# Another order of the steps in a linear-attention and feed-forward kernel

## The chip, the cores and the metric

One core of a Trainium2 chip runs the whole program. The metric is the device time of that core in microseconds (us). Five engines work side by side, each through its own list of instructions in a fixed order: PE (TensorE: matrix products; its weight loads are shown as PEld), DVE (VectorE), ACT (ScalarE), POOL (GpSimd) and SP (SyncE, which issues nearly all DMAs here). An instruction that waits holds up everything behind it on its engine.

## The reference

```python
# attention: q, k, v, alpha of shape (4, 8, 768, 48)
for t in range(S):
    state = alpha[:, :, t, :, None] * state + einsum('bhd,bhe->bhde', k[:, :, t], v[:, :, t])
    y[:, :, t] = einsum('bhd,bhde->bhe', q[:, :, t], state)
# feed-forward: x = y as (3072 tokens, 384); w_in (384, 2048), w_out (2048, 384)
h = x @ w_in
sp = maximum(h, 0.0) + log1p(exp(-abs(h)))
out = (h * erf(sp)) @ w_out
```

The inputs are float64; the result is float32.

## The kernel before, in words

The 768 positions are cut into 12 chunks of 64. A chunk holds 64 positions of all four batches, 256 tokens, and after the attention of a chunk a feed-forward block of the same number works on its 256 tokens. The work is written as named steps; a step is a generator, and each time that its name comes in the table `SCHED` it issues one piece. Names end in numbers: `y_1` is step `y` of chunk 1; `H_7_2_0` is step `H` of block 7, group 2, half 0; `wi_5` and `wo_5` are tile 5 of `w_in` and of `w_out` (16 tiles each).

Attention steps of chunk n:
- `la`, `lk`, `lq`, `lv` load alpha, keys, queries and values (SP). `kx`, `qx` copy rows of K and Q to a fourth block (SP, line 236).
- `a1` is the running product of alpha (DVE, L353); `ln`, `ex`, `gd` take its logarithm, its inverse and a range check (ACT); `w1`, `w2`, `w3`, `a3` scale K and Q (DVE).
- `s` multiplies queries with keys (PE, L414) and masks the result into `sT` (DVE). `t` turns the keys (PE, L434) and copies them into `kn` (line 211 on ACT or 213 on DVE); `u` adds keys times values to the state `T` (PE L462, DVE L470).
- `lv`/`tx` and `qc`/`sx` gather values with state into W and queries with `sT` into X by DMA (L301, L334, L314, L324). `y` multiplies X with W (PE, L504) and writes the block's input: `x_hi` by a copy, `x_lo` as the rest.

Feed-forward steps of block n, for four groups of four tiles each:
- `H` is `x @ w_in` in three products of high and low halves, 12 and then 6 matmuls (L590), and a copy of the PSUM bank into `hs`. Block 0 instead takes `w_in` whole in fp32 (L579).
- `U`, `L1` (three), `G` are five ACT instructions on 128x1024 values; `U` and `G` need another table of functions than `L1`, `ln` and `ex`, and each change costs an ACT_TABLE_LOAD (L204). `L2` and `Z` are two DVE instructions each.
- `O` copies the result to `gh` (ACT or DVE), makes `gl` (DVE), and then issues 12, 12, 6 and 6 matmuls with `w_out` (L660) that add to two PSUM banks `acc`. `out` copies these and sends them off.

A weight tile arrives as float64 in a buffer `wst`, and steps `wi`, `wo` of seven pieces each turn it into a high and a low float32 half: one DMA, a copy and a shift (mostly ACT, L211 and L710), two DVE instructions (L714, L718), the copy to `wi_hi` or `wo_hi`, and the DVE subtraction to `wi_lo` or `wo_lo` (L726).

What sets the order: `steps()` walks through `SCHED` and issues piece by piece, and PE, ACT, DVE and SP keep exactly that order. A prefix `v:` puts a copy of that piece on DVE instead of ACT (for a third piece of `wi` or `wo` it is the other way: the shift goes to ACT). Big tiles share 24 buffers of 4 KB per partition, PSUM is eight banks; a piece waits until its buffer is free.

Of the kernel before, what the change touches and what calls it, by code (L numbers as in the profile page):

```python
# [44 lines left out]
a3_1 wi_6 qx_1 H_0_0_1 wi_13 wi_14 v:wi_14 w3_2 wi_15 wi_9 wi_6 wi_2 wi_1 wi_7 wi_14 wi_6 H_0_1_0 H_0_0_0 wi_0 t_2
U_0_0 u_0 v:wi_9 wi_14 wi_14 kx_2 a3_2 wi_7 wi_12 wi_12 wi_6 wi_8 wi_13 v:wi_13 u_0 wi_2 s_1 wi_8 s_1 H_0_1_1 wi_10
qx_2 H_0_3_1 s_1 wi_9 wi_13 v:wi_12 wi_12 wi_13 v:wi_8 wi_8 wi_5 s_2 lv_1 wi_10 H_0_1_0 v:wi_10 wi_7 H_0_1_1 v:wi_13
wi_7 wi_12 t_2 v:t_2 wi_11 tx_1 wi_8 wi_10 sx_1 qc_1 wi_14 U_0_1 wi_12 wi_12 v:wi_8 wi_9 wi_8 wo_9 la_3 wi_11 v:wi_11
u_1 L1_0_1 s_2 wi_11 wi_10 wi_13 L1_0_0 wi_11 L1_0_0 H_0_3_0 wo_4 v:H_0_3_0 wi_10 s_2 wo_5 u_1 L1_0_0 L1_0_1 H_0_2_0
L2_0_0 a1_3 wi_11 y_1 wi_10 y_1 y_1 y_1 wi_9 H_0_2_1 wi_9 wo_3 wo_0 L1_0_1 H_0_2_0 wo_9 v:wo_9 H_1_0_0 ln_3 H_1_3_0  # L50
sx_2 wi_11 wo_9 H_0_2_1 y_1 wo_5 qc_2 wo_9 wo_3 H_1_1_0 H_1_1_1 L2_0_1 ex_3 y_1 H_1_0_0 L2_0_0 H_0_3_1 lv_2 wo_4
L2_0_1 tx_2 v:wo_5 wo_5 G_0_0 H_1_1_0 H_1_1_0 G_0_1 H_1_1_1 wo_0 H_1_2_1 v:wo_4 w1_3 H_1_1_1 H_1_3_0 y_2 wo_5 wo_5
w2_3 v:wo_3 v:wo_0 lk_3 Z_0_1 wo_2 u_2 w3_3 Z_0_0 lq_3 wo_3 wo_15 wo_4 y_2 a3_3 H_1_3_0 H_1_0_0 U_0_3 wo_4 wo_3 Z_0_1
wo_15 wo_0 t_3 t_3 t_3 H_1_0_1 y_2 y_2 v:wo_15 wo_4 wo_3 u_2 kx_3 wo_2 wo_1 wo_4 wo_1 y_2 y_2 wo_6 qx_3 wo_3 wo_15
v:wo_1 L1_0_3 H_1_2_1 H_1_0_1 H_1_2_0 H_1_3_1 wo_9 wo_5 H_1_2_0 s_3 lv_3 u_3 la_4 tx_3 wo_14 wo_1 v:wo_2 v:H_1_0_1
wo_6 wo_1 H_1_2_0 H_2_2_0 s_3 wo_6 s_3 wo_0 wo_9 wo_1 wo_1 qc_3 H_1_3_1 L1_0_3 wo_6 wo_15 H_1_2_1 Z_0_0 H_2_0_0
H_1_3_1 L1_0_3 H_2_2_1 H_2_1_1 O_0_1 u_3 sx_3 H_2_2_0 wo_0 wo_14 v:wo_14 wo_0 U_1_0 wo_8 L2_0_3 G_0_3 wo_10 wo_15
H_2_0_0 y_3 H_2_2_0 y_3 wo_6 O_0_0 L2_0_3 a1_4 wo_10 v:wo_10 wo_15 H_2_3_1 wo_2 H_2_1_1 H_2_0_0 y_3 O_0_0 Z_0_3 U_0_2
wo_7 wo_2 wo_14 wo_7 v:wo_7 wo_7 wo_13 O_0_0 wo_10 H_2_2_1 H_2_2_1 y_3 H_2_0_1 H_2_3_1 wo_2 H_3_2_1 y_3 wo_2 wo_8 gd_3
wo_14 y_3 wo_6 wo_13 O_0_0 wo_11 v:wo_8 la_5 wo_10 lk_4 Z_0_3 v:wo_10 v:wo_11 v:wo_11 H_3_2_1 wo_7 O_0_1 wo_10 H_2_0_1  # L60
ln_4 wo_8 wo_6 O_0_0 H_2_1_0 L1_0_2 H_3_2_1 wo_7 ex_4 wo_7 ends_3 wo_11 wo_14 H_2_3_1 w1_4 v:wo_13 wo_13 wo_8 H_2_3_0
w2_4 lq_4 H_3_3_1 wo_13 L1_0_2 O_0_0 H_3_2_0 L1_1_0 a3_4 O_0_1 ends_3 w3_4 L1_0_2 H_3_2_0 wo_13 wo_14 L1_1_0 wo_13
O_0_1 L2_0_2 H_3_2_0 qx_4 wo_12 H_2_3_0 L1_1_0 H_3_3_0 H_2_1_0 O_0_1 wo_11 wo_8 wo_8 L2_0_2 u_3 H_3_3_0 kx_4 H_2_0_1
H_2_3_0 v:wo_12 G_0_2 Z_0_2 O_0_1 H_3_3_1 H_2_1_0 wo_11 wo_11 qc_4 v:wo_12 t_4 lv_4 H_2_1_1 H_3_3_1 Z_0_2 L2_1_0 U_1_1
tx_4 s_4 s_4 s_4 O_0_2 H_3_0_1 O_0_2 O_0_2 H_3_0_0 L2_1_0 H_3_3_0 wo_12 G_1_0 L1_1_1 t_4 Z_1_0 L1_1_1 t_4 O_0_2 wo_12
H_3_0_1 O_0_3 O_0_2 Z_1_0 u_4 L1_1_1 U_2_0 sx_4 y_4 v:wo_12 O_0_3 U_1_3 H_3_0_0 O_0_2 y_4 wo_12 L2_1_1 u_4 O_0_3 O_1_0
L2_1_1 lk_5 a1_5 G_1_1 O_1_0 y_4 O_1_0 O_0_3 v:y_4 Z_1_1 U_1_2 O_1_0 la_6 O_0_3 lq_5 O_1_0 ln_5 tx_5 v:H_3_0_1 O_0_3
L1_1_3 ex_5 L1_1_2 O_1_0 Z_1_1 O_1_1 w1_5 L1_2_0 out_0_1 H_4_0_0 y_4 y_4 w2_5 O_1_1 w3_5 O_1_1 L1_2_0 H_4_2_1 out_0_1
O_1_1 H_4_2_1 v:out_0_0 out_0_0 L1_1_2 H_4_2_0 L1_2_0 L1_1_2 a3_5 qx_5 L2_2_0 L2_1_2 L2_2_0 L1_1_3 L1_1_3 L2_1_2
H_4_0_0 G_1_2 U_2_2 lv_5 L2_1_3 H_3_0_0 kx_5 O_1_1 H_4_2_0 H_4_2_0 G_1_3 H_4_0_1 O_1_1 t_5 v:H_4_2_1 s_5 Z_1_2 v:t_5  # L70
t_5 Z_1_2 u_5 U_2_1 s_5 G_2_0 s_5 Z_2_0 H_4_0_1 O_1_2 L2_1_3 H_3_1_0 H_3_1_1 u_5 qc_5 Z_1_3 L1_2_2 L1_2_1 O_1_2 O_1_2
H_4_3_0 H_3_1_1 H_4_3_0 sx_5 H_3_1_0 Z_1_3 L1_2_2 O_1_2 L1_2_2 H_4_0_0 L1_2_1 L1_2_1 H_4_0_1 Z_2_0 y_5 v:H_3_1_0
L2_2_2 H_3_1_1 O_2_0 U_3_1 y_5 L2_2_2 v:H_4_3_0 v:O_1_3 L2_2_1 G_2_2 H_4_1_1 U_3_0 lq_6 O_1_2 G_2_1 H_4_1_1 O_2_0
O_2_0 O_1_2 U_2_3 L1_2_3 y_5 L1_2_3 L2_2_1 O_2_0 Z_2_1 Z_2_1 O_1_3 O_1_3 L1_3_0 y_5 O_2_0 O_1_3 v:O_2_1 O_2_1 y_5
L1_3_0 L1_3_0 H_4_3_1 O_1_3 Z_2_2 v:H_4_1_1 O_2_0 L1_2_3 Z_2_2 H_4_3_1 a1_6 O_2_1 L1_3_1 L1_3_1 O_1_3 H_5_2_0 O_2_1
out_1_0 L1_3_1 y_5 L2_2_3 U_3_3 H_4_3_1 H_5_2_0 L2_3_0 H_5_2_1 O_2_2 H_4_1_0 L2_3_1 G_3_0 O_2_1 out_1_0 H_5_3_0 G_3_1
G_2_3 L2_3_0 v:out_1_1 Z_3_0 L2_2_3 O_2_1 O_2_2 H_5_3_1 U_4_0 L2_3_1 O_2_2 H_4_1_0 Z_3_0 Z_2_3 a3_6 U_3_2 L1_3_2 gd_5
Z_3_1 L1_3_3 ln_6 H_5_3_0 O_3_0 O_2_2 Z_2_3 H_5_3_1 H_4_1_0 H_5_3_1 qx_6 ex_6 H_5_0_0 lk_6 L1_3_2 O_2_2 O_2_3 O_3_0
O_3_0 Z_3_1 O_2_2 w1_6 out_1_1 L1_3_2 O_3_0 L1_3_3 O_3_1 L1_3_3 O_2_3 O_2_3 L2_3_2 H_5_2_1 H_5_2_1 O_2_3 L2_3_2 O_3_0
O_2_3 L2_3_3 G_3_2 lv_6 L1_4_0 w2_6 H_5_3_0 w3_6 H_5_2_0 O_3_0 O_2_3 out_2_0 Z_3_2 O_3_1 O_3_1 L2_3_3 la_7 H_5_1_0  # L80
O_3_1 t_6 v:out_2_1 L1_4_0 L1_4_0 Z_3_2 v:t_6 t_6 gd_6 kx_6 s_6 u_6 L2_4_0 G_4_0 qc_6 s_6 s_6 L2_4_0 U_4_1 O_3_1 G_3_3
H_5_0_0 tx_6 H_5_0_1 O_3_1 O_3_2 a1_7 L1_4_1 L1_4_1 H_5_1_0 Z_3_3 Z_4_0 ln_7 Z_4_0 lq_7 gd_4 H_5_1_1 H_5_1_0 L1_4_1
O_3_2 O_3_2 H_5_0_1 u_6 Z_3_3 O_3_2 v:O_3_3 sx_6 O_4_0 H_5_1_1 O_3_2 L2_4_1 y_6 lk_7 H_5_0_0 y_6 y_6 y_6 y_6 O_4_0
O_4_0 O_3_2 lv_7 ex_7 tx_7 w1_7 O_4_0 y_6 w2_7 L2_4_1 U_4_3 G_4_1 la_8 O_3_3 Z_4_1 Z_4_1 O_3_3 U_5_2 O_4_0 O_3_3
H_5_1_1 U_4_2 L1_4_2 out_2_0 L1_4_3 L1_4_2 H_6_3_1 ends_7 O_3_3 H_6_0_1 O_3_3 out_3_1 out_3_1 L1_4_3 w3_7 O_4_0 a1_8
H_6_3_0 H_6_3_1 kx_7 H_6_0_1 v:O_4_1 ln_8 O_4_1 out_3_0 a3_7 L1_4_2 L2_4_2 H_6_0_0 O_4_1 L1_4_3 H_6_0_0 O_4_1 out_2_1
v:H_6_0_1 L2_4_2 lq_8 H_6_3_0 ex_8 qx_7 O_4_1 t_7 L2_4_3 G_4_2 Z_4_2 out_3_0 ends_7 H_6_0_0 a3_8 H_5_0_1 qc_7 U_5_1
s_7 H_6_3_1 v:t_7 t_7 U_5_0 G_4_3 L1_5_1 Z_4_2 O_4_2 u_7 u_7 lk_8 L1_5_1 H_6_3_0 O_4_1 s_7 s_7 H_6_2_0 L2_4_3 L1_5_2
w1_8 w2_8 H_6_1_0 w3_8 H_6_1_1 O_4_2 O_4_2 L1_5_1 H_6_2_0 u_7 H_6_1_0 O_4_2 la_9 t_8 H_6_2_0 H_6_1_0 L1_5_0 L1_5_0
sx_7 L2_5_1 y_7 L1_5_0 y_7 y_7 L2_5_1 Z_4_3 v:y_7 lv_8 G_5_1 H_6_1_1 gd_7 L2_5_0 G_5_0 kx_8 qx_8 y_7 tx_8 y_7 O_4_2  # L90
U_5_3 Z_4_3 O_4_3 H_7_0_0 H_7_0_1 L2_5_0 Z_5_0 O_4_2 H_6_2_1 Z_5_1 H_7_0_1 U_6_0 H_7_0_0 O_4_3 v:t_8 qc_8 O_4_3 Z_5_0
Z_5_1 H_6_2_1 L1_5_3 t_8 H_7_1_1 v:H_7_0_1 L1_6_0 O_5_0 O_4_3 H_7_1_1 v:H_6_2_1 O_4_3 H_6_1_1 v:H_7_0_0 O_5_0 s_8 s_8
s_8 u_8 O_5_0 u_8 H_7_1_0 O_5_0 L1_5_3 L1_5_3 L1_5_2 L1_5_2 L2_5_2 L1_6_0 L2_5_3 H_7_3_0 L2_5_3 L1_6_0 sx_8 L2_6_0
G_5_3 L2_5_2 L2_6_0 O_5_0 G_5_2 H_7_1_1 G_6_0 Z_6_0 O_4_3 H_7_1_0 H_7_1_0 O_5_0 Z_5_2 U_6_2 a1_9 y_8 y_8 H_7_3_0
# [863 lines left out]
```

## Time and profile before

| what | value |
|---|---|
| time of the kernel, median of 3 runs | 507.15 us (503.38 to 513.17) |
| the profiled execution's own time | 503.65 us |
| its span, first to last instruction | 501.9 us |
| busy PE / DVE / ACT | 470.8 / 463.3 / 456.8 us |
| ACT_TABLE_LOADs | 46, of 1283 ns each |
| mean granted TensorE clock | 0.994 |

The span is the time between the first and the last instruction of the profiled execution; its own time is 1.75 us longer. Busy time is the time in which an engine works on at least one instruction. Two instructions of an engine overlap a little in the records (a 128x1024 ACTIVATE is recorded at 1053 ns, while the next one starts 950 ns after it), so what an instruction adds to a queue is read from start to start. An engine can be busy and still be held up by another before or after; the chain of waits tells which engine's work ended last.

### The profile page before, as it was taken

To read this page: it belongs to the slowest core of one execution; us is meant where nothing else is said; L and a number is where in the kernel's file an instruction comes from. 1 tells how busy PE (TensorE), PEld (TensorE's weight loads), DVE (VectorE), ACT (ScalarE), POOL (GpSimd) and SP (SyncE) were. 2 spreads that over 40 slices of the span, in tenths; PEclk is the share of its full clock that TensorE was granted. 3 is DMA by queue.
4 is the path that set the end of the run, shared out by engine and by line. 5 is a ranking of instruction groups with operands and counts; after the bars stand their busy time and mean duration, and the time that the engine had idled before them with its cause. 6 is when DMAs were issued, how large, how long until landed. Compare 5 with 4: busy or idle time off the path is not lost.

```text
span 501.9 us, 15223 instructions
## 1 busy us (share of the span) xinstructions
PE 470.8 (94%) x6484; PEld 458.8 (91%) x6484; DVE 463.3 (92%) x579; ACT 456.8 (91%) x610; POOL 12.1 (2%) x50
## 2 busy tenths in 40 slices
...
DMA packets 37370, 58.68 MB, mean 117 GB/s; under 512 B 4848, under 2 KB 23152, under 8 KB 37296
## 3 DMA queue, kind: packets, MB, share of 16 engines
...
q8 instruction: 53, 0.87, 0.8%
q14 instruction: 21, 0.17, 0.1%
...
## 4 chain that ended last, share of the span: by engine, by line
PE 55%; ACT 20%; DVE 10%; DMA 9%; issue 4%; SPq 1%; DVEq 0%; ACTq 0%
PE acc L660 28%; PE ph L590 21%; ACT s L205 5%; ACT w L205 3%; PE py L504 2%; ACT L204 2%; ACT hs L211 2%; DMA W<-T 2%; DMA W<-in_v_dram 1%; ACT gh L211 1%; DMA X<-sT 1%; PE pS L414 1%; DMA wst<-in_moe_w_in_dram 1%; DMA X<-Q 1%; PE pu L462 1%
## 5 line engine op out<-in xcount | busy, mean ns | idle before, releaser
L660 PE MATMUL acc<-gh,wo_hi 128*128 128x256 f32 x576 | 135.5, 278 | 0.0
L660 PE MATMUL acc<-gh,wo_lo 128*128 128x256 f32 x576 | 135.1, 277 | 0.0
L590 PE MATMUL ph<-x_hi,wi_hi 128*128 128x256 f32 x528 | 124.9, 279 | 0.9 <-issue 0.7
L590 PE MATMUL ph<-x_hi,wi_lo 128*128 128x256 f32 x528 | 123.9, 277 | 0.0
L660 PEld LDWEIGHTS acc<-gh,wo_hi 128*128 128x128 f32 x576 | 108.2, 188 | 0.4 <-ACT hs L211 0.2
L660 PEld LDWEIGHTS acc<-gh,wo_lo 128*128 128x128 f32 x576 | 108.2, 188 | 0.0
L590 PEld LDWEIGHTS ph<-x_hi,wi_hi 128*128 128x128 f32 x528 | 99.2, 188 | 1.1 <-issue 0.4
L590 PEld LDWEIGHTS ph<-x_hi,wi_lo 128*128 128x128 f32 x528 | 99.2, 188 | 0.9 <-issue 0.8
L205 ACT ACTIVATE s<-s 128x1024 f32<-128x1024 f32 x96 | 99.5, 1053 | 0.4
L660 PE MATMUL acc<-gl,wo_hi 128*128 128x256 f32 x576 | 77.7, 278 | 0.0
L590 PE MATMUL ph<-x_lo,wi_hi 128*128 128x256 f32 x528 | 71.5, 278 | 0.0
L660 PEld LDWEIGHTS acc<-gl,wo_hi 128*128 128x128 f32 x576 | 70.9, 188 | 0.4
L590 PEld LDWEIGHTS ph<-x_lo,wi_hi 128*128 128x128 f32 x528 | 65.0, 188 | 0.4
L620 DVE TENSOR_TENSOR t<-s,w 128x1024 f32<-128x1024 f32 x48 | 57.9, 1221 | 8.0 <-ACT w L205 5.8
L631 DVE TENSOR_TENSOR s<-s,w 128x1024 f32<-128x1024 f32 x48 | 58.3, 1221 | 3.9 <-ACT s L205 3.4
L204 ACT ACT_TABLE_LOAD x46 | 59.0, 1283 | 1.6 <-PEq L905 0.8
L644 DVE TENSOR_TENSOR gl<-hs,gh 128x1024 fp32r<-128x1024 f32 x48 | 58.3, 1219 | 0.7 <-ACT gh L211 0.2
L633 DVE SCALAR_TENSOR_TENSOR hs<-s,hs 128x1024 f32<-128x1024 f32 x48 | 58.3, 1220 | 0.3
L622 DVE SCALAR_TENSOR_TENSOR w<-t,w 128x1024 f32<-128x1024 f32 x48 | 57.9, 1220 | 0.4
L205 ACT ACTIVATE s<-hs 128x1024 f32<-128x1024 f32 x48 | 49.5, 1052 | 2.8 <-DVE s L631 2.4
L205 ACT ACTIVATE w<-s 128x1024 f32<-128x1024 f32 x48 | 50.5, 1054 | 1.1 <-PE acc L660 0.6
L205 ACT ACTIVATE w<-w 128x1024 f32<-128x1024 f32 x48 | 50.0, 1055 | 0.5
...
## 6 DMA issues: line engine op xcount, KB each, us to landing
...
```

The lines of the kernel that those rows point to most:

```text
L204: nc.scalar.preload_act_table_set(table)
L205: nc.scalar.activation(*args, **kw)
L211: nc.scalar.activation(out, in_, AF.Copy, scale=scale)
L414: nc.tensor.matmul(out=ps[half][i * TC : (i + 1) * TC, pair * M + m, :], lhsT=K[rows, pair, m, i, :], rhs=Q[rows, pair, i, m, :], start=Tr ...
L504: nc.tensor.matmul(out=py[i][c0 : c0 + 32, kt, m, :], lhsT=left[r0 : r0 + rows, l0 : l0 + 32], rhs=right[r0 : r0 + rows], start=kt == m == ...
L590: nc.tensor.matmul(out=ph[:, u * self.TB : (u + 1) * self.TB].rearrange("p (a t) -> p a t", t=CT), lhsT=wt[:, kt, fs], rhs=xt[:, at, kt], ...
L620: nc.vector.tensor_tensor(out=t, in0=s, in1=w, op=ALU.mult)
L622: nc.vector.scalar_tensor_tensor(out=w, in0=t, scalar=2.0, in1=w, op0=ALU.add, op1=ALU.mult)
L631: nc.vector.tensor_tensor(out=s, in0=s, in1=w, op=ALU.mult)
L633: nc.vector.scalar_tensor_tensor(out=h, in0=s, scalar=RT2 / 2, in1=h, op0=ALU.subtract, op1=ALU.mult)
L644: nc.vector.tensor_tensor(out=gl, in0=h, in1=gh.bitcast(F32), op=ALU.subtract)
L660: nc.tensor.matmul(out=self.acc[dm // n][:, dm % n * self.TB : (dm % n + 1) * self.TB], lhsT=wt[:, f, dm * P : (dm + 1) * P], rhs=gt[:, c0 ...
```

## The change

The table `SCHED` is replaced by another one of the same 1653 names: each step occurs as often as before, and no other line differs. What differs is the order and which copies carry `v:`. So the matmuls and the DMAs are the same in number and size. 84 pieces carry `v:` instead of 95. With the order the table loads become 48 instead of 46. Counted in the table's positions, the last three `w_out` tiles were finished at 476 (tile 8), 490 (tile 11) and 535 (tile 12) before and are finished at 507 (tile 12), 511 (tile 15) and 531 (tile 14) now; tile 14 moved from 461 to 531 and tile 15 from 379 to 511. The first two products of block 1 stood at 230 and stand at 229 (of another half) and 264 (half 0 of group 0).

```diff
--- before.py
+++ after.py
@@ -37,97 +37,97 @@
 SCHED = """
-la_0 la_0 la_1 a1_0 ln_0 a1_0 a1_1 ln_0 lq_0 a3_0 a3_0 wi_2 ex_0 w1_0 ex_0 w1_0 lk_0 la_2 w2_0 lk_1 wi_5 w2_0 ln_1
-w3_0 w3_0 gd_1 s_0 ex_1 w1_1 gd_0 qx_0 qx_0 t_0 a1_2 wi_3 w2_1 wi_2 v:wi_2 kx_0 kx_0 s_0 lv_0 t_0 s_0 w3_1 wi_5 t_1
...
+la_0 la_0 a1_0 la_1 wi_4 a1_0 a1_1 ln_0 ex_0 w1_0 lq_0 lk_0 wi_1 la_2 a3_0 wi_6 a3_0 ln_0 ex_0 w1_0 ln_1 w2_0 w2_0
+wi_4 v:wi_4 gd_0 w3_0 w3_0 ex_1 w1_1 v:wi_1 wi_6 v:wi_6 wi_0 v:wi_1 qx_0 a1_2 ln_2 wi_0 gd_1 qx_0 wi_5 w2_1 s_0 wi_5
...
```

The first place is SP's queue at the start of the program behind the first three loads of alpha (`wst` is a weight tile; the first Q and K are chunk 0's, a second K is chunk 1's). Before:

```order
L270 DMA Q<-in_qk_dram 128x768
L705 DMA wst<-in_moe_w_in_dram 128x768
L259 DMA K<-in_qk_dram 128x768
L251 DMA A<-in_alpha_dram 128x780
L259 DMA K<-in_qk_dram 128x768
L705 DMA wst<-in_moe_w_in_dram 128x768
L236 DMA Q<-Q 48x1x256 x2
```

And now:

```order
L705 DMA wst<-in_moe_w_in_dram 128x768
L270 DMA Q<-in_qk_dram 128x768
L259 DMA K<-in_qk_dram 128x768
L705 DMA wst<-in_moe_w_in_dram 128x768
L251 DMA A<-in_alpha_dram 128x780
L705 DMA wst<-in_moe_w_in_dram 128x768 x2
L236 DMA Q<-Q 48x1x256 x2
```

Four `w_in` tiles instead of two are asked for ahead of the copy of Q's rows, and the keys of chunk 1 have gone from here to a place behind the values of chunk 0. The first load of Q now stands behind one `w_in` tile.

The second place is ACT where it copies group 0 of block 7 to `gh` (`gh_5356<-hs_4220` before, `gh_5207<-hs_4632` now, the 447th instruction of ACT's list in both). Before:

```order
L204 ACT_TABLE_LOAD
L205 ACTIVATE s_4947<-s_4947 128x1024
L205 ACTIVATE r_5319,flags_82<-r_5319 128x768
L211 ACTIVATE hs_5352<-ph_5035 128x512
L211 ACTIVATE gh_5356<-hs_4220 128x1024
L211 ACTIVATE hs_5361<-ph_5066 128x512
L205 ACTIVATE w_5235<-w_5235 128x1024
```

And now:

```order
L204 ACT_TABLE_LOAD
L205 ACTIVATE s_4832<-s_4832 128x1024
L211 ACTIVATE x_hi_97<-py_5088 128x3x128
L211 ACTIVATE x_hi_97<-py_5089 128x3x128
L211 ACTIVATE gh_5207<-hs_4632 128x1024
L211 ACTIVATE hs_5026<-ph_4837 128x512
L205 ACTIVATE s_5219<-hs_5026 128x1024
L204 ACT_TABLE_LOAD
```

The copy of block 7 stands at the same place of ACT's list, but other work stands around it: the input of block 9 (`x_hi`) is already copied ahead of it, and the ACT work on block 8 follows behind it.

The third place is ACT at the last copies to `wo_hi`. Before:

```order
L205 ACTIVATE s_1466<-s_1466 128x1024
L211 ACTIVATE hs_1788<-ph_1593 128x512
L211 ACTIVATE wo_hi_91<-wst_1554 128x384
L710 ACTIVATE wst_1722<-wst_1722 128x384
L211 ACTIVATE hs_1788<-ph_1317 128x512
```

And now:

```order
L211 ACTIVATE gh_1798<-hs_846 128x1024
L204 ACT_TABLE_LOAD
L205 ACTIVATE s_1739<-s_1739 128x1024
L211 ACTIVATE wo_hi_91<-wst_1728 128x384
L205 ACTIVATE w_1893<-s_1739 128x1024
L205 ACTIVATE w_1893<-w_1893 128x1024
```

The last such copy on ACT went from the 182nd to the 193rd row of the list.

## Rows read from the trace of the kernel before

**Rows 1.** The page: span, and busy time of each engine with its share.

```profile
span 501.9 us, 15223 instructions
PE 470.8 (94%) x6484; PEld 458.8 (91%) x6484; DVE 463.3 (92%) x579; ACT 456.8 (91%) x610; POOL 12.1 (2%) x50
```

**Rows 2.** Busy time in three stretches; columns as in the first row.

```profile
core 0: us, PE busy (x) PEld busy (x) DVE busy (x) ACT busy (x) POOL busy (x), PEclk, DMA share, GB/s
0.00:256.10 256.10, 233.71 (x3432) 224.30 (x3435) 237.75 (x334) 239.13 (x356) 9.91 (x41) 0.99 0.61 161
256.10:354.60 98.50, 98.24 (x1465) 96.58 (x1456) 93.78 (x105) 94.66 (x115) 2.06 (x8) 1.00 0.42 109
354.60:494.70 140.10, 138.66 (x1601) 137.80 (x1600) 131.20 (x140) 122.41 (x140) 0.12 (x1) 1.00 0.17 41
```

**Rows 3.** Chain of waits, parts: start us, us, engine, tile and line, instructions.

```profile
256.33 0.98 PE pu L462 x63
258.19 4.08 PE ph L590 x36
262.27 1.36 PE acc L660 x12
...
294.67 2.00 PE py L504 x124
...
452.63 41.95 PE acc L660 x370
```

**Rows 4.** Timeline of ACT at the turned keys of chunk 7: start, us, instruction.

```profile
255.44 0.70 ACT L211 ACTIVATE kn<-pn 128x288 f32<-128x288 f32 x2
```

**Rows 5.** Timeline of ACT at block 7's first `gh`.

```profile
352.27 0.83 ACT L205 ACTIVATE r<-r 128x768 f32<-128x768 f32 x1
...
353.09 0.58 ACT L211 ACTIVATE hs<-ph 128x512 f32<-128x512 f32 x1
353.57 1.05 ACT L211 ACTIVATE gh<-hs 128x1024 fp32r<-128x1024 f32 x1
```

**Rows 6.** Waits of ACT from 256.1 to 354.6 us: total, times, longest.

```profile
ACT o L211 <- DMA X<-Q: 1.6, 1, 1.6
ACT w L205 <- PE acc L660: 0.6, 1, 0.6
ACT hs L211 <- PE ph L590: 0.4, 1, 0.4
ACT kn L211 <- PE pn L434: 0.3, 1, 0.3
ACT s L205 <- PE pS L414: 0.2, 1, 0.2
```

**Rows 7.** Timeline of ACT at a table load and at an `x_hi` copy.

```profile
176.38 1.05 ACT L205 ACTIVATE s<-hs 128x1024 f32<-128x1024 f32 x1
177.44 1.28 ACT L204 ACT_TABLE_LOAD   x1
178.74 1.06 ACT L205 ACTIVATE s<-s 128x1024 f32<-128x1024 f32 x1
179.70 0.47 ACT L211 ACTIVATE x_hi<-py 128x384 fp32r<-128x384 f32 x1
180.07 1.05 ACT L205 ACTIVATE w<-s 128x1024 f32<-128x1024 f32 x1
```

**Rows 8.** Timeline of ACT in the first 60 us; the bracket is the idle time before.

```profile
20.45 0.57 ACT L211 ACTIVATE wst<-wst 128x384 f32<-128x384 f32 x1 [1.79 <-DMA wst<-in_moe_w_in_dram]
46.60 0.57 ACT L211 ACTIVATE wst<-wst 128x384 f32<-128x384 f32 x1 [2.34 <-DMA wst<-in_moe_w_in_dram]
47.07 0.54 ACT L710 ACTIVATE wst<-wst 128x384 int32<-128x384 uint32 x1
57.26 0.87 ACT L211 ACTIVATE x_hi<-py 128x384 fp32r<-128x384 f32 x2 [2.47 <-PE py L504]
```

**Rows 9.** Timeline of PE at its first instruction.

```profile
11.55 1.14 PE L414 MATMUL pS<-Q,K 48*64 48x64 f32 x32 [11.55 <-DVE K L392]
```

More of the change, by code (lines that the diff above doesn't have):

```diff
@@ L45 @@
[L45 to L94, printed above, removed]
@@ L105 @@
-O_7_0 w2_10 lk_11 H_8_2_0 L1_7_3 w3_10 L1_7_2 w2_11 w3_11 out_6_1 out_6_1 H_9_2_1 a3_10 L1_7_2 H_9_0_1 gd_10 L2_7_2
-out_6_0 G_7_2 L2_7_3 H_9_2_1 O_7_0 H_9_0_0 kx_10 O_7_0 H_9_2_0 L2_7_3 gd_11 H_9_0_0 H_8_1_1 H_9_0_0 O_7_0 kx_11 L2_7_2
-H_8_2_1 qx_11 H_9_2_0 t_10 out_6_0 H_8_1_1 qx_10 H_9_0_1 G_7_3 tx_10 Z_7_2 s_10 v:H_9_2_1 v:t_10 s_11 t_10 U_8_1 Z_7_2
-s_10 u_10 O_7_0 qc_10 s_10 H_9_1_0 Z_7_3 v:O_7_1 v:O_7_2 O_7_0 U_9_0 u_10 U_8_0 L1_8_0 s_11 sx_10 Z_7_3 s_11 H_9_1_1
-L1_8_0 O_7_1 L1_8_1 L1_8_1 L1_8_1 L2_8_1 O_7_1 y_10 L1_8_0 y_10 H_9_1_0 H_9_1_0 H_9_3_1 O_7_1 L1_9_0 H_9_3_0 L1_9_0
@@ new lines @@
+v:wi_15 wi_9 t_1 v:wi_3 lq_1 v:wi_3 wi_14 v:wi_14 wi_7 wi_14 wi_15 t_1 wi_0 wi_6 wi_3 wi_15 wi_3 wi_9 v:wi_9 wi_5 wi_1
+wi_15 wi_2 wi_13 a3_1 wi_13 wi_1 wi_7 wi_12 kx_1 wi_0 wi_10 wi_9 wi_6 lq_2 wi_14 H_0_0_0 u_0 v:wi_2 wi_2 H_0_1_1
+v:wi_13 qx_1 lk_2 u_0 H_0_1_0 H_0_0_0 wi_12 s_1 wi_7 wi_3 wi_2 wi_11 wi_10 H_0_0_1 lv_1 v:wi_10 wi_10 v:wi_12 wi_12
+wi_14 w3_2 wi_10 la_3 qc_1 H_0_3_1 wi_12 u_1 H_0_1_1 U_0_1 s_1 wi_13 s_1 wi_8 wi_9 t_2 wi_15 wi_13 H_0_3_0 tx_1 wi_11
+v:wi_11 wi_11 wi_3 wi_12 H_0_0_1 U_0_0 a3_2 a1_3 wi_2 wi_11 wi_12 H_0_2_1 L1_0_1 sx_1 wi_10 wi_10 wi_9 L1_0_0 wi_9
@@ new lines @@
+qx_2 wi_11 wi_11 v:H_0_3_1 u_1 kx_2 wi_2 y_1 wi_13 wi_8 wo_4 v:wi_8 wi_14 wi_8 wo_3 lk_3 wi_13 ln_3 wi_8 ex_3 t_2 wo_5
+L1_0_1 lq_3 wo_0 L1_0_1 s_2 wi_8 y_1 y_1 v:t_2 w1_3 w2_3 H_0_2_0 y_1 L2_0_1 L1_0_0 H_1_0_1 y_1 y_1 w3_3 tx_2 L2_0_1
+gd_3 lv_2 wo_5 v:wo_5 wo_5 wi_8 ends_3 H_0_3_0 L1_0_0 H_1_1_1 H_0_2_1 s_2 qc_2 wo_5 s_2 sx_2 L2_0_0 wo_0 kx_3 H_1_0_1
+wo_4 H_1_2_1 v:wo_4 wo_4 G_0_1 wo_9 v:wo_0 wo_3 H_0_2_0 H_1_0_0 a3_3 H_1_2_0 Z_0_1 H_1_1_1 L2_0_0 H_1_2_0 wo_5 H_1_0_0
+wo_5 qx_3 G_0_0 H_1_2_0 wo_2 wo_6 U_0_3 L1_0_3 Z_0_0 Z_0_0 wo_11 H_1_0_1 wo_4 H_1_2_1 wo_9 u_2 u_2 v:wo_9 y_2 y_2 y_2
@@ new lines @@
+H_3_3_1 Z_1_0 v:wo_14 H_3_3_1 v:wo_12 t_4 t_4 wo_15 v:wo_15 Z_0_2 t_4 qc_4 O_0_2 u_3 s_4 L1_1_1 s_4 s_4 lv_4 H_3_2_0
+H_3_1_1 wo_15 wo_15 wo_12 wo_14 wo_15 Z_1_0 wo_15 O_0_2 O_0_2 L1_1_1 L1_1_1 L2_1_1 tx_4 H_3_2_1 H_3_0_0 U_2_0 wo_14
+O_0_2 L2_1_1 H_3_0_0 U_1_2 v:wo_14 u_4 u_4 O_0_2 G_1_1 wo_14 H_3_2_0 O_0_2 Z_1_1 O_0_3 H_3_0_1 a1_5 U_1_3 v:O_1_0
+H_3_1_1 v:H_3_2_0 L1_1_3 L1_2_0 sx_4 y_4 O_0_3 y_4 Z_1_1 O_0_3 H_3_0_1 y_4 v:y_4 ln_5 H_3_0_0 ex_5 y_4 w1_5 L1_2_0
+L1_1_3 O_1_0 O_0_3 H_3_0_1 O_1_0 O_0_3 O_1_0 L1_1_3 w2_5 L2_1_3 lk_5 O_0_3 L1_1_2 H_4_0_1 O_1_0 O_1_1 w3_5 lq_5 a3_5
```

108 lines of the change are left out of this document (74 added, 34 removed).

## The prediction

> **What bounds the kernel now.** I read the page's totals first, then the chain of waits, then the stretches, then ACT's and PE's rows where the chain changes hands. The totals [rows 1] show three engines nearly full: PE 470.8 us of a span of 501.9, DVE 463.3, ACT 456.8. The reader is to see that no engine has more than 45 us to give away, and that the PE work is the same in any order, so PE's idle time decides.
>
> In the chain [rows 3], PE holds nearly every piece from 256 us to the end. It takes over from ACT at one place: ACT ends the copy of chunk 7's keys at 256.1 us (255.44 + 0.70) [rows 4], and the matmuls `u_7` that read it start at 256.33 [rows 3]. After that PE is busy 98.24 of 98.5 us, then 138.66 of 140.1 [rows 2]. The last matmul ends at 494.6 us (452.63 + 41.95) [rows 3]. The stores and the closing check take 7.3 us more, to 501.9. So the span is 256.1 us of ACT (its work and its waits), 238.3 us of PE, 7.3 us of end.
>
> The time is a profiled one: 503.65 us for this execution, 1.75 more than its span, and the median of the three runs is 507.15, another 3.5 higher. The sum below is made on the span, and 5.25 us are added at the end.
>
> **The prices.** From start to start a 128x1024 ACT instruction takes 0.96 us (178.74 to 179.70). A table load takes 1.30 (177.44 to 178.74), and the instruction ahead of it loses its overlap of 0.10, so 1.4. `x_hi` takes 0.37 (179.70 to 180.07) [rows 7], a `ln` or `ex` 0.82 (352.27 to 353.09), a copy of half a group 0.48 (353.09 to 353.57) [rows 5], a weight copy 0.47 (46.60 to 47.07) [rows 8], two key copies 0.70 [rows 4]. On PE a set of 12 feed-forward matmuls takes 1.36 us, a set of 6 half of it; 62 to 64 matmuls of `u` take 0.98, 124 of `y` 2.00 [rows 3].
>
> As a check, count the PE work behind `u_7` in the table of before: 104 sets of 12 (141.4), 105 of 6 (71.4), 10 halves of `y` (10.0), 4 each of `u` and `s`, 3 of `t` (some 11): 234 us. The trace shows 238.3. PE therefore loses 1.8% on counted work, and I use that factor.
>
> **The change, part by part.** The table decides which work stands ahead of a point on ACT and which PE work still stands behind it. I counted this at every place where PE reads a product of ACT. In the old order the sum is largest at `u_7`, and falls after it. In the new order it is within about 2 us of its largest value at `O_3_0`, `O_4_1`, `O_5_2`, `O_7_0` and `u_10`, and is largest at `O_7_0`: ACT stays the limiter for about 90 us longer. So the sum goes through `O_7_0`.
>
> - ACT ahead of `gh` of `O_7_0`, new against old: one table load fewer (-1.4), two weight copies fewer (-0.9), one `ln` and one `ex` fewer (-1.6), one 128x1024 fewer (-0.96), one `x_hi` fewer (-0.4), two pairs of key copies more (+1.4), one copy of block 0's input more (+0.4), two output copies more (+0.8). Together -2.7 us. The old `gh` ended at 354.6 [rows 5]; the new one would end at 351.9.
> - PE work behind it: the table has 8 more sets of 12 (+10.9) and 6 more sets of 6 (+4.1): block 8's first products are not made yet. That is 147.6 us of counted work instead of 132.6, and with the factor 150.3.
> - ACT's waits between 256 and 354.6: 3.1 us, four of the five directly for PE, the fifth ahead of a copy of PE's sums [rows 6]. There ACT was ahead. Where ACT is the limiter they should go. Ends: all of it or nothing; I take all, since in the new order PE is the one that lags. 348.8.
> - The start. ACT waits 1.8 and 2.3 us for `w_in` tiles and 2.5 us for `y_1` [rows 8]. The new queue asks for four `w_in` tiles before Q's rows are copied instead of two, and the last tile is asked for 36 positions ahead of its first use instead of 15. The wait of 2.3 is nearest to this and I take it as gone; its cover is those 36 positions. Ends: all 6.6 us gone, or as much again added, because Q, K and the tiles share one queue.
> - Copies moved to ACT: 11 fewer pieces carry `v:`, so DVE gets lighter by about 7 us and ACT by two loads and these copies heavier by about 8. Ahead of `O_7_0` this is in the count above; behind it PE alone is on the chain, so the rest costs nothing as long as PE lags. If that cover is gone, ACT's products for block 11 are late next.
> - The late `w_out` tiles 12 to 15 cost nothing: the last is finished at position 531, and `O_0_3`, which reads them, starts its matmuls at 549. The same distance was 3 positions before. Their cover is `O_0_2` and the products of blocks 2 and 3. Without it, PE would wait at `O_0_3` for the copy, the subtraction and a matmul, by an estimate from these prices at most 2 us.
> - The start of PE at 11.55 [rows 9] moves by about one tile's transfer at most, since one `w_in` tile goes ahead of Q and the keys; DVE's chain, not Q, ended that wait, so nothing.
>
> Sum: 348.8 - 2.3 + 150.3 + 7.3 = 504.1 us of span, 2.2 more than before. With 1.75 it is 505.9, with the 3.5 of the median **509 us**, 0.4% slower. If the 3.1 and the 2.3 both stay, 509.5 of span, 515 on the median's scale.
>
> The Trainium skill, page "ScalarE: Activation LUTs", section "What ACT_TABLE_LOAD costs", gives a load of about 1283 ns and a drain of about 1380 ns for each change of table, 2.66 us together, and would thus speak against an order with two more loads. Here the load is 1.28 us, but it starts 0.01 us after the instruction ahead of it ends, and the next starts 0.02 us after the load [rows 7]: no such drain shows on this path. By the page the load fewer ahead of `O_7_0` would be worth 1.3 us more, and the sum 508; the measured row decides.
>
> **The rivals.**
> *A smoother start.* Old ACT waits of 1.8, 2.3 and 2.5 us [rows 8] all go. For it: five tiles are asked for by the time that three were. Against: what the tiles gain the keys of chunk 1 lose. The time: 504.1 - 4.3 = 499.8 of span, 505 on the median's scale, 0.4% faster.
>
> *A late chunk 1 (the other side).* The keys of chunk 1 stood ahead of the second `w_in` tile and now stand behind the fifth and the values of chunk 0; its queries stand behind eleven tiles instead of eight. Its chain is K and Q, `s_1`, the gathers into X, `y_1`, and then `x_hi` on ACT, in order, with the rest of ACT behind it. Already now ACT waits 2.5 us there [rows 8]. Each us by which X comes later is a us of ACT, and ACT's path has none to spare before `O_7_0`. A delay of 10 us gives 506.4 (without the gain of 2.3) + 10 - 1.2 (more ACT work ahead of it now) = 515 of span, 520 on the median's scale, 2.6% slower. It decides from a wait of about 8 us at that copy.
>
> *PE alone.* If ACT's waits before `O_7_0` shrink by over 5 us more, ACT no longer limits anywhere and PE's own waits go as well. PE works 470.8 us [rows 1]; with its first 11.55 [rows 9] and the end of 7.3 the floor is 489.7. Half the way from 499.8 to there is 495, 500 on the median's scale; over 2% faster needs 492.
>
> *No real change*, since steps and sizes are the same: 507. This lies between the forecast and the smoother start and is counted with them.
>
> **How the numbers follow.** A measurement of this kernel tells about 2% from no change: its three runs lie within -0.7% and +1.2% of the median. Forecast (505 to 515 on the median's scale) 0.42; smoother start (500 to 505) 0.25; late chunk 1 or another wait of its size (over 517) 0.22; PE nearly without waits (under 497) 0.11. So faster by over 2% 0.11, within 2% 0.67, slower 0.22. The range reaches down to 498, past the smoother start, and up to 521, the late chunk 1 with its 10 us; about one in ten is left out on each side.
>
> **What would show it.** In the new profile ACT's first `gh` of block 7 should end near 346.5 us, and the chain should name ACT until about there instead of 256, and PE after it. The wait of 2.3 us for a `w_in` tile near 46 us should be gone; a wait of over 8 us at block 1's `x_hi` would be the late chunk. ACT should be busy about 464 us, DVE 456, PE 471, with 48 loads of 1.28 us. I am wrong if PE is on the chain well before 340 us, or if PE's first 120 us hold clearly more or less idle time than before.

## The result and the profile after

The changed kernel took 514.85 us in the median of six runs (510.78 to 520.81), the kernel before 508.39 beside it (503.38 to 513.17). The ratio is **1.0126, with a 95% interval of 1.0088 to 1.0163**: slower by 1.3%, which is inside 2%. Run a second time on another occasion it came out at 1.0184 (1.0064 to 1.0304). The forecast was 509 us and 0.4%.

The first profile of the changed kernel was of a disturbed execution (span 519.0 us), so the rows of "after" are those of the second one, span 509.5. Its page, answering to [rows 1]:

```profile
span 509.5 us, 15222 instructions
PE 470.0 (92%) x6484; PEld 458.2 (90%) x6484; DVE 456.1 (90%) x566; ACT 464.1 (91%) x625; POOL 11.7 (2%) x50
...
q8 instruction: 53, 0.87, 0.8%
...
L204 ACT ACT_TABLE_LOAD x48 | 61.6, 1283 | 1.6 <-PEq L905 0.8
```

PE works as long as before, 470.0 us, and the span is 7.6 us longer: PE is idle more. ACT is up by 7.3 us and DVE down by 7.2, as the 48 loads and the moved copies said. Where PE is idle is read from stretches; here those of the kernel before, with PE's busy time as the second number:

```profile
0.00:125.00 125.00, 102.68 (x1651) 95.22 (x1652) 110.63 (x190) 108.88 (x197) 6.55 (x29) 0.99 0.82 226
125.00:250.00 125.00, 124.93 (x1677) 123.15 (x1677) 121.10 (x136) 124.22 (x151) 3.24 (x11) 1.00 0.38 95
250.00:317.00 67.00, 66.74 (x1014) 65.36 (x1013) 64.80 (x75) 65.26 (x80) 0.84 (x4) 1.00 0.39 105
317.00:360.00 43.00, 43.00 (x596) 42.55 (x595) 40.33 (x46) 40.82 (x53) 1.33 (x5) 1.00 0.47 119
360.00:400.00 40.00, 38.56 (x720) 37.81 (x718) 37.23 (x44) 37.63 (x44) 0.12 (x1) 1.00 0.47 105
```

and of the changed one:

```profile
0.00:125.00 125.00, 99.63 (x1642) 93.08 (x1643) 112.12 (x191) 110.68 (x200) 6.67 (x30) 0.99 0.83 227
125.00:250.00 125.00, 122.84 (x1772) 120.39 (x1771) 117.41 (x136) 123.20 (x151) 2.19 (x9) 1.00 0.40 101
250.00:317.00 67.00, 66.94 (x908) 65.76 (x906) 64.63 (x71) 65.98 (x83) 1.46 (x6) 1.00 0.35 94
317.00:360.00 43.00, 40.78 (x571) 40.26 (x572) 39.43 (x43) 41.63 (x53) 1.22 (x4) 1.00 0.36 99
360.00:400.00 40.00, 37.55 (x589) 36.95 (x589) 33.15 (x38) 35.22 (x43) 0.12 (x1) 0.96 0.60 124
```

The reader is to see three places: 3.1 us more idle time up to 125 us, 2.1 more up to 250, and 3.2 more between 317 and 400 (2.22 + 2.45 - 1.44). The last is the odd one, since there PE alone is on the chain. The chain of waits of the changed kernel (start, length, what) shows it, and what stands around it:

```profile
315.64 1.46 ACT hs L211 x3
317.15 1.17 PE pS L414 x62
...
341.65 1.12 PE py L504 x61
342.77 1.08 PE pu L462 x64
343.85 1.10 PE py L504 x60
344.95 0.44 PE acc L660 x2
345.39 2.07 issue
...
371.19 2.10 PE pS L414 x126
373.29 0.64 PE pu L462 x42
373.93 2.45 issue
376.38 0.62 PE pu L462 x21
377.01 2.86 PE acc L660 x12
379.86 2.93 PE ph L590 x24
...
472.88 29.03 PE acc L660 x256
```

Twice PE stops in the middle of a set ("issue": it waits for nothing that the profile shows), at the end of a long run of small matmuls: right behind `y_9`, `u_9`, `y_9`, 192 in a row, and inside the last part of `t_10`, `s_11`, `s_10`, `u_10`, 198 in a row. After the second stop 12 feed-forward matmuls take 2.86 us instead of 1.36, because the clock was granted at half, the lower of its two levels (1.2 GHz), behind the stop and at full before and after; PEclk is the third number from the right:

```profile
370.00:373.90 3.90, 3.90 (x182) 3.64 (x180) 2.97 (x6) 3.48 (x8) 0.00 (x0) 1.00 1.14 175
376.70:380.10 3.40, 3.40 (x30) 3.31 (x22) 1.87 (x4) 3.37 (x5) 0.00 (x0) 0.50 0.54 135
380.10:386.00 5.90, 5.90 (x53) 5.90 (x53) 5.58 (x6) 3.97 (x4) 0.00 (x0) 1.00 0.24 67
```

The matmuls of that stretch lose 1.7 us (2.86 - 1.36, and 2.93 - 2.72). Together 6.2 us stand at these two places. The kernel before has one such stop, of 1.44 us at 368.5, in its own run of 198, and keeps the full clock there; so 4.8 of the 7.6 us come from here.

What moved: in the old order `u_n` mostly stands behind `s_n`, and the two halves of `y_n` follow later, runs of 128 and 134. In the new order `u` (or `s`) stands between the halves of `y` at `y_1`, `y_3`, `y_5`, `y_6` and `y_9`, and `u_2` right ahead of both halves of `y_2`: runs of 192. (Before, only `y_2` with `u_2` and `t_3`, and the `t_10` run, 198 each. Chunk 0 has a run of 204 in both orders.)

### The profile page after: what moved, and what is told of

It reads as the page before. It is cut to its first block, busy times and chain, and to the rows that moved or that the text cites. A ratio compares the mean times of both kernels' runs of the same rounds, so it can differ in the third digit from the quotient of the medians.

```text
span 519.0 us, 15222 instructions
## 1 busy us (share of the span) xinstructions
PE 478.6 (92%) x6484; PEld 466.3 (90%) x6484; DVE 456.1 (88%) x566; ACT 464.9 (90%) x625; POOL 11.7 (2%) x50
## 4 chain that ended last, share of the span: by engine, by line
PE 52%; ACT 18%; DVE 11%; DMA 9%; issue 7%; SPq 3%; ACTq 0%; DVEq 0%
PE acc L660 24%; PE ph L590 21%; ACT s L205 6%; ACT w L205 3%; PE py L504 3%; ACT L204 2%; DMA wst<-in_moe_w_in_dram 2%; DMA X<-Q 2%; DVE s L631 2%; DVE w L622 2%; ACT hs L211 2%; DMA X<-sT 2%; PE pu L462 1%; PE pS L414 1%; DMA Q<-Q 1%
## 5 line engine op out<-in xcount | busy, mean ns | idle before, releaser
L660 PE MATMUL acc<-gh,wo_hi 128*128 128x256 f32 x576 | 139.2, 282 | 0.0
L660 PE MATMUL acc<-gh,wo_lo 128*128 128x256 f32 x576 | 137.9, 280 | 0.0
L660 PEld LDWEIGHTS acc<-gh,wo_hi 128*128 128x128 f32 x576 | 109.4, 190 | 0.7
L660 PEld LDWEIGHTS acc<-gh,wo_lo 128*128 128x128 f32 x576 | 109.4, 190 | 0.0
L660 PE MATMUL acc<-gl,wo_hi 128*128 128x256 f32 x576 | 80.3, 280 | 1.5 <-issue 1.5
L660 PEld LDWEIGHTS acc<-gl,wo_hi 128*128 128x128 f32 x576 | 72.6, 188 | 2.0 <-issue 1.6
L211 ACT ACTIVATE hs<-ph 128x512 f32<-128x512 f32 x79 | 45.0, 589 | 6.6 <-PE ph L590 6.4
```

What stands on the lines that cost most here:

```text
L211: nc.scalar.activation(out, in_, AF.Copy, scale=scale)
L660: nc.tensor.matmul(out=self.acc[dm // n][:, dm % n * self.TB : (dm % n + 1) * self.TB], lhsT=wt[:, f, dm * P : (dm + 1) * P], rhs=gt[:, c0 ...
```

## The experiments

Theory 1: ScalarE (ACT) limits longer. Theory 2: the new start loses the time. After the first four runs came theory 3: in long runs of small matmuls TensorE (PE) outruns the delivery of its own instructions; and after e8 theory 4: it is where `u` stands, by its buffers and what waits for it. Ratios are to the kernel before, with 95% intervals.

| run | ratio |
|---|---|
| e1 changed kernel again | 1.0184 (1.0064 to 1.0304) |
| e2 kernel before again | 1.0019 (0.9974 to 1.0064) |
| e3 old start, new rest | 1.0136 (0.9959 to 1.0312) |
| e4 new start, old rest | 1.0112 (1.0068 to 1.0156) |
| e5 late runs apart | 1.0047 (1.0013 to 1.0082) |
| e6 less ACT work | 1.0113 (1.0057 to 1.0170) |
| e7 all but two runs apart | 0.9987 (0.9947 to 1.0028) |
| e8 old with long runs | 1.0130 (1.0083 to 1.0176) |
| e9 big sets between | 1.0035 (1.0003 to 1.0067) |
| e10 old, its runs apart | 1.0022 (0.9988 to 1.0056) |
| e11 e7 and `u_2` apart | 1.0004 (0.9972 to 1.0037) |
| e12 new start, runs apart, old rest | 1.0080 (1.0046 to 1.0114) |

**Controls.** No edit in either.

> The changed kernel as it is, for a second profile. Both theories expect +1.0 to +1.6% against the kernel before. Theory 1 (ACT limits longer in the steady part): PE's idle time in the first 125 us as before (22 us, give or take 2), ACT's gh of block 7 group 0 ends at 347 to 352 us, and the chain names ACT until 320 us or later. Theory 2 (the start loses the time): PE is idle 25 us or more in the first 125 us, and from 125 us to the end no more idle than before (9 us).

> The kernel before as it is, for a second profile: ratio 1.00, within 0.4%. PE idle 22 us in the first 125 us and 9 after them, if the first profile of it was typical; a PE wait of over 3 us on its own issue in the start would show that such waits come by chance.

Both came out as the kernels that they are; the difference is real. The signs in e1's trace are split: PE is idle 25.4 us up to 125 us, as theory 2 said, but 14.1 us behind that, not 9; `gh` of block 7 ends at 347.1 us, as theory 1 said, but the chain leaves ACT at 317. In e2 PE is idle 20.6 us up to 125 us and 8.8 behind that, without a long wait on its own issue.

**Start or rest.** The first 536 steps of the old table followed by the others in the new order, and the reverse with 532:

```diff
-SCHED = new order of all 1653 steps
+SCHED = old[:536] + (the other steps, in the new order)      # e3
+SCHED = new[:532] + (the other steps, in the old order)      # e4
```

> The first 536 steps of the old table (until the last w_out tile is converted), then what is left in the new table's order. 48 table loads. Theory 1 (steady part): as slow as the change, +1.0 to +1.6%. Theory 2 (start): the loss is gone, -0.3 to +0.3%.

> The first 532 steps of the new table, then what is left in the old table's order. 46 table loads. Theory 1 (steady part): no loss, -0.3 to +0.3%. Theory 2 (start): +1.0 to +1.6%.

e4 was slower by 1.1%, where theory 1 had no loss. e3's 1.4% has an interval that takes in no change, so its time decides nothing. A hybrid also has a wait at its own seam, which is no part of either kernel. Waits of PE in e4 from 130 to 150 us (total, times, longest), where neither whole kernel has any:

```profile
PE acc L660 <- DVE hs L213: 1.5, 1, 1.5
```

So the two times don't say in which half the loss lies. The traces gave the next theory: both kernels with the new rest have the two stops near 350 and 375 us and the half clock behind the second one (e3: 1.4 and 3.0 us), and e4, with the old rest, has none near 350.

**Late runs apart.** `u_9` and `u_10` are moved behind full-size matmuls; nothing is added or left out.

```diff
-lv_9 y_9 G_7_1 u_9 u_9 Z_7_1 y_9 y_9 ... O_6_3 O_7_0 O_6_3 ln_11
+lv_9 y_9 G_7_1 Z_7_1 y_9 y_9 ... O_6_3 O_7_0 O_6_3 u_9 u_9 ln_11
-s_10 u_10 qc_10 U_8_1 ... s_10 O_7_1 s_10 H_8_2_1 Z_8_0
+s_10 qc_10 U_8_1 ... s_10 O_7_1 s_10 H_8_2_1 u_10 Z_8_0
```

> The changed kernel, with two steps of TensorE moved in the part that TensorE limits: u_9 goes out from between the two halves of y_9 to behind O_6_2, H_8_3_0 and O_6_3, and u_10 goes from behind t_10, s_11 and s_10 to behind O_7_1 and H_8_2_1. The two runs of 192 and 198 small matmuls in a row become runs of 128 and 134; no instruction is added or taken away. Theory 3 (in long runs of small matmuls TensorE outruns the delivery of its own instructions: 2.07 us at 345.4 us and 2.45 us at 373.9 us in the changed kernel's trace, and the half clock at 376.7 to 380.1 us, worth 1.7 us, follows the second): both waits and the half clock go, 4 to 6 us less than the changed kernel, +0.2 to +0.8% against the kernel before. Theory 1 (ScalarE stays the limit up to 317 us) and theory 2 (the start): within 1 us of the changed kernel, +1.0 to +1.6%.

+0.5%, as theory 3 said; the interval ends at 0.8%, below what theories 1 and 2 allowed. All of PE's waits from 320 to 400 us, and the stretch with its clock:

```profile
PE pu L462 <- issue: 0.3, 1, 0.3
```
```profile
360.00:400.00 40.00, 39.69 (x619) 38.92 (x618) 36.91 (x43) 38.96 (x48) 0.12 (x1) 1.00 0.61 127
```

Of 4.5 us of stops 0.3 are left, and the clock stays full.

**Less ACT work.** In blocks 4 and 5 the Exp of `L1` is left out, so these two blocks compute something else.

```diff
-            act(LNEXP, w, w, AF.Exp, scale=-1.0)
+            if self.n not in (4, 5):
+                act(LNEXP, w, w, AF.Exp, scale=-1.0)
```

> The changed kernel without the third activation of L1 (the Exp) in blocks 4 and 5: eight ScalarE instructions of 1.04 us, 8.3 us of ScalarE between some 250 and 320 us, are left out, so those two blocks compute something else; nothing else is touched. Theory 1: ScalarE is what TensorE waits for up to about 317 us, so most of it comes back until VectorE, as busy, limits: 3 to 6 us less than the changed kernel, about +0.2 to +0.7% against the kernel before, and the chain of waits goes over to TensorE near 270 us. Theories 2 and 3: under 1.5 us less, +0.9 to +1.5%, and the waits near 345 and 374 us stay.

+1.1%, against 1.3% of the changed kernel: from leaving out 8.3 us of ACT's work no gain shows beyond the noise. The interval reaches down to 0.6%, into theory 1's range, so the time alone doesn't exclude it. The stops stayed (PE's waits, 320 to 400 us; the edit moved the line numbers by one):

```profile
PE pu L462 <- issue: 2.7, 1, 2.7
PE acc L661 <- issue: 1.9, 1, 1.9
```

What speaks against theory 1 most plainly stands in the stretches above: the chain names ACT up to 317 us, but from 250 to 317 PE is busy 66.94 of 67.00 us, so ACT's work there has nothing to give back. Two engines are tied, and the chain names one of them.

**All but two runs apart.** As e5, and four more:

```diff
-L1_0_1 s_2 wi_8 y_1 y_1 v:t_2 w1_3 w2_3 H_0_2_0 y_1
+L1_0_1 wi_8 y_1 y_1 v:t_2 w1_3 w2_3 H_0_2_0 s_2 y_1
-H_2_2_1 y_3 ... U_0_2 u_3 wo_2
+u_3 H_2_2_1 y_3 ... U_0_2 wo_2
-O_1_3 O_1_3 y_5 u_5 U_3_1
+O_1_3 u_5 O_1_3 y_5 U_3_1
-w1_7 O_3_2 y_6 ... U_4_1 u_6 y_6
+w1_7 u_6 O_3_2 y_6 ... U_4_1 y_6
```

> As the run before with the two steps of TensorE moved (u_9, u_10), and four more: s_2 goes out from between the halves of y_1, u_5 and u_6 from between those of y_5 and y_6, u_3 from between those of y_3; only two runs over 134 small matmuls are left, those of chunk 0 and of y_2. Theory 3: also the 2.7 us of issue time at 75 us go, 5 to 8 us less than the changed kernel, -0.3 to +0.6% against the kernel before. Theory 1: within 1 us of the changed kernel. Theory 2 (the start loses TensorE time for its own reasons): as the run with u_9 and u_10 alone.

-0.1%, with an interval of 0.4% on either side: the loss is gone, in the new order. Over e5 it gains 0.6%, which the intervals, that overlap, only just tell from nothing. PE's busy time from 125 to 250 us rises from 122.84 in the changed kernel to 124.55:

```profile
125.00:250.00 125.00, 124.55 (x1785) 122.44 (x1784) 119.02 (x138) 123.51 (x151) 2.19 (x9) 1.00 0.41 103
```

One expectation failed: the stop near 75 us stayed (2.33 us). There `u_2` and the two halves of `y_2` still stand in one run, the one that was not broken.

**The old order with long runs.** The suspected cost put in:

```diff
-t_5 Z_1_2 u_5 U_2_1 ... H_3_1_1 u_5 qc_5 ... y_5 L2_2_2 v:H_4_3_0
+t_5 Z_1_2 U_2_1 ... H_3_1_1 qc_5 ... u_5 y_5 u_5 L2_2_2 v:H_4_3_0
-v:t_9 u_9 U_7_3 ... sx_9 u_9 out_5_0 ... y_9 y_9 L1_7_1
+v:t_9 U_7_3 ... sx_9 out_5_0 ... y_9 u_9 y_9 u_9 L1_7_1
```

> The kernel before, with the suspected cost put in: u_5 and u_9 moved in between the two halves of y_5 and y_9, as the changed kernel has them, so two runs of 134 and 128 small matmuls become two of 70 and 192 each. Theory 3: a wait of 1 to 3 us for instructions at y_9 (near 345 us), where TensorE limits, and the same at y_5 near 215 us in part hidden by ScalarE: +0.3 to +0.8% against the kernel before. Theories 1 and 2: no change, within 0.3%.

+1.3%, over the range that theory 3 gave, and by another cause. PE's timeline at `y_9` (start, length, instruction, idle time before and what ended it):

```profile
339.65 1.15 PE L504 MATMUL py<-X,W 128*32 128x64 f32 x62 [0.73 <-DMA X<-sT]
340.73 0.31 PE L462 MATMUL pu<-W,kn 64*64 64x48 f32 x2
342.95 1.95 PE L462 MATMUL pu<-W,kn 64*64 64x48 f32 x62 [1.91 <-ACT hs L211]
```

`u_9` waits for a copy on ACT that empties its PSUM bank, and behind that wait the clock falls to half (0.50 from 342.8 to 346.2 us). At this place the waits of 0.73 and 1.91 us and some 1.4 us for 126 small matmuls at half clock can be read (1.95 and then 1.75 us, where e9 below has 1.15 and 1.17), 4.0 us of a span that is 6.9 us longer; where the rest went is open. The run doesn't test the length, because moving `u` also made it wait for its bank.

**Length alone.** Hence a kernel in which `y`, `s`, `t` and `u` keep their order, and full-size matmuls are brought forward between them:

```diff
-y_9 G_7_1 u_9 u_9 Z_7_1 y_9 ... O_6_2 ... H_8_3_0 ... O_6_3 O_7_0
+y_9 G_7_1 O_6_2 H_8_3_0 u_9 u_9 Z_7_1 O_6_3 O_7_0 y_9
-s_10 u_10 qc_10 ... O_7_1 s_10 H_8_2_1
+O_7_1 s_10 H_8_2_1 u_10 qc_10 ... s_10
```

> The changed kernel with y, s, t and u left in their order, and full-size matmuls brought forward between them: two sets of 6 (O_6_2, H_8_3_0) before u_9, two sets of 12 (O_6_3, O_7_0) before the second half of y_9, one of 12 (O_7_1) before s_10 and one of 12 (H_8_2_1) before u_10. So the runs of 192 and 198 are broken without u_9 or u_10 being moved against y and s. Theory 3 (the length of the run): as the run with u_9 and u_10 moved: the waits of 2.07 and 2.45 us near 345 and 374 us and the half clock behind them go, 3 to 6 us less than the changed kernel, +0.3 to +0.8% against the kernel before. Theory 4 (it is where u stands, by its buffers and what waits for it, and not the length): the loss stays, +1.0 to +1.6%.

+0.35%, as theory 3 said, and below theory 4's range. PE's timeline at `y_9`, without a stop:

```profile
343.13 1.38 PE L504 MATMUL py<-X,W 128*32 128x64 f32 x64
344.44 0.96 PE L660 MATMUL acc<-gl,wo_hi 128*128 128x256 f32 x6
345.24 0.84 PE L590 MATMUL ph<-x_lo,wi_hi 128*128 128x256 f32 x6
346.01 1.15 PE L462 MATMUL pu<-W,kn 64*64 64x48 f32 x64
347.09 1.17 PE L504 MATMUL py<-X,W 128*32 128x64 f32 x64
```

In the changed kernel's timeline the same three sets start at 341.58, 342.70 and 343.78, 1.1 us apart: 128 instructions (a weight load and a matmul each) in 1.1 us. A feed-forward set takes 24 instructions in 1.36 us. The edit did less than the expectation says: the two pieces put before the second half of `y_9` hold no matmuls (they are the copy to `gh` and the making of `gl`), so 12 big matmuls stand ahead of `u_9`, and `u_9` and that half still follow each other, 128 in a row. At `s_10` and `u_10` the trace has a set of 12 between each two parts, as intended. The waits of 2.07 and 2.45 us are both gone.

**The rest.** Both kernels with more runs broken, and the new start with its three runs broken ahead of the old rest:

```diff
-y_2 wo_5 ... Z_0_1 wo_2 u_2 w3_3 ... y_2 ... H_1_0_1 y_2          # e10, old order
+y_2 wo_5 ... Z_0_1 wo_2 w3_3 ... y_2 ... H_1_0_1 u_2 y_2
-s_10 u_10 O_7_0 qc_10 s_10 H_9_1_0
+s_10 O_7_0 qc_10 s_10 H_9_1_0 u_10
-u_2 u_2 v:wo_9 y_2 y_2 ... H_1_1_0 t_3                            # e11 (e7 with this), e12 (e4 with this,
+v:wo_9 y_2 y_2 ... H_1_1_0 u_2 t_3 u_2                            # and s_2, u_3 as in e7)
```

> The kernel before, with its own two runs of 198 small matmuls broken: u_10 moved from behind t_10, s_10 and s_11 to behind O_7_0 and H_9_1_0, u_2 from between the halves of y_2 to behind H_1_0_1. Theory 3: the wait of 1.44 us at 368.5 us goes and little else (no wait stood at y_2 in the trace of before): 1 to 2 us less, -0.4 to -0.2% against the kernel before. Theory 4: no change, within 0.2%.

> As the run in which all but two long runs were broken, and u_2 also moved, from before y_2 to behind H_1_1_0, so that only the run of chunk 0 is left. Theory 3: the 2.33 us of issue time at 77 us, which stood right behind u_2 and y_2 there, go; of them at most 2 us reach the end, since ScalarE limits right after: -0.5 to 0.0% against the kernel before. Theory 4: as that run, -0.3 to +0.2%.

> The new start with the old rest (its first 532 steps in the changed kernel's order, +1.1% when run as it was), with the three runs of 192 small matmuls in that start broken: s_2 moved from between the halves of y_1 to behind H_0_2_0, u_2 from before y_2 to behind H_1_1_0, u_3 from between the halves of y_3 to before H_2_2_1. Theory 3: what the new start lost was in these runs (2.34 us of issue time at 78.4 us, 1.54 us at 145.7 us and the half clock at 79.2 to 82.6 us in that kernel's trace): 3 to 5 us less than it, -0.1 to +0.5% against the kernel before. Theory 2 (the start loses the time by the order of its weight tiles): no change, +0.7 to +1.5%.

e10 missed: the stop of 1.44 us went (0.5 us of another wait is left there), but the time did not fall; a gain of 1.4 us is within this interval of 0.7%. e11 is as e7 within the noise. In its trace the stop of 2.33 us near 75 us is gone (from 60 to 130 us PE has one stop of 1.8 us, where e7 has two, 3.8 together), but a wait of 2.8 us, put down to DVE's work on a weight tile, has come in, and the clock is at 0.95 up to 125 us, so what breaking the `y_2` run is worth can't be read from it. e12 missed as well: 0.8% where theory 3 allowed 0.5. Its expectation took e4's wait of 1.54 us at 145.7 us for a part of the long runs, but that is the seam, which breaking runs doesn't touch. Here the seam is larger, with half clock behind it:

```profile
PE acc L660 <- DVE hs L213: 2.0, 1, 2.0
```
```profile
125.00:150.00 25.00, 23.00 (x345) 22.20 (x345) 21.13 (x28) 19.81 (x25) 0.61 (x2) 0.93 0.40 100
```

Both whole kernels are busy all 25 us there. e7 and e11 have the new start and the new rest and are level with the kernel before within 0.4%, so with the runs broken no loss of the new start shows. No version was faster than the kernel before by more than the noise.

## Why the prediction was nearly right

**ACT to the first `gh` of block 7** was forecast to end near 346.5 us; it ended at 347.1 (346.03 + 1.06):

```profile
346.03 1.06 ACT L211 ACTIVATE gh<-hs 128x1024 fp32r<-128x1024 f32 x1
```

The count of ACT instructions ahead of it is right, and the 3.1 us of ACT's waits [rows 6] taken as gone are gone: no wait of ACT is named from 256.1 to 354.6 us now. That the sum is so near is in part luck. The stretch up to `gh`, in the kernel before and in the changed one (ACT's busy time is the fourth number behind the length):

```profile
0.00:354.60 354.60, 331.95 (x4883) 320.88 (x4884) 331.52 (x438) 333.79 (x470) 11.97 (x49) 1.00 0.55 147
0.00:347.10 347.10, 317.64 (x4776) 306.94 (x4777) 321.84 (x423) 329.78 (x469) 10.93 (x47) 1.00 0.54 145
```

ACT's idle time fell by 3.5 us (20.8 to 17.3) and not by the 5.4 of the sum, and its busy time by 4.0 us and not by the 2.7 of the priced count; the two misses nearly cancel.

**The start.** The wait of 2.34 us for a tile near 46 us [rows 8] is 0.68 now, and `x_hi` of block 1 waits 2.41 instead of 2.47; the rival of the late chunk 1 didn't come. (The other wait for a `w_in` tile went from 1.79 to 1.6 us, and two waits for `w_out` tiles, 1.1 us together, are new. The late `w_out` tiles 12 to 15 cost PE nothing: it has no wait for one from 125 to 320 us.)

```profile
48.45 0.54 ACT L211 ACTIVATE wst<-wst 128x384 f32<-128x384 f32 x1 [0.68 <-DMA wst<-in_moe_w_in_dram]
...
56.87 0.87 ACT L211 ACTIVATE x_hi<-py 128x384 fp32r<-128x384 f32 x2 [2.41 <-PE py L504]
```

**PE behind `gh`**: this term failed in its size. The sum had 150.3 us, the counted matmuls times 1.018; measured are 154.8, from 347.1 to 501.9 (472.88 + 29.03). Of these, 147.6 are the counted work and 6.2 the two stops and the half clock; the factor had allowed 2.7 for all waits. In e9, which breaks just these runs, `gh` ends at 347.73 (346.69 + 1.04) and the last matmul at 498.19, 150.5 us later, the number of the forecast:

```profile
346.69 1.04 ACT L211 ACTIVATE gh<-hs 128x1024 fp32r<-128x1024 f32 x1
```
```profile
469.16 29.03 PE acc L660 x256
```

So the span of 504.1 missed 509.5 by 0.6 at `gh`, 4.5 behind it and 0.3 in the end and roundings. The factor came from one stretch of the old order, where small matmuls stand in runs of 128 to 134 and one of 198; it didn't hold for an order with a run of 192 more. The stop of 1.44 us in the old trace was there to be seen, and would have given a first price: no rival named it. That the prediction gives just 509.5 for the case in which ACT's waits both stay is chance: the waits mostly went, and PE lost the time.

**What was to show it** held for busy times and loads. But both signs of being wrong came. PE was to come on the chain near 346 us and not well before 340; it came at 317. The picture of ACT alone as the limit up to `O_7_0` was too simple: PE loses 0.06 us from 250 to 317, and its matmuls on that `gh` start at 348.60, 1.5 us after the copy ends:

```profile
348.60 0.28 PE L660 MATMUL acc<-gh,wo_hi 128*128 128x256 f32 x1
```

Without the stop of 2.07 us PE would have been there at 346.5, 0.6 us before the copy's end: the engines were tied, so a sum along ACT's path and one along PE's come out alike. And the first 125 us hold 3.1 us more PE idle time, with a stop of 2.7 behind the run of `u_2` and `y_2` (waits of PE, 60 to 130 us; before, all such stops there came to 1.2):

```profile
PE ph L590 <- issue: 2.7, 1, 2.7
```

The range was wide enough because the rival of a late chunk 1 stretched it, not because this cause was in it.
